# Seven block products in the second unit's first pair, row blocks loaded by SyncE, and a drain behind every two-source GpSimd operation

## The chip, the core and the metric

One core of a Trainium2 chip. The metric is the device time of one execution in microseconds. The kernel before took 782.65 us (median of three runs, 782.61 to 783.22). Engines are named as in the profile: PE is TensorE's matmuls and PEld its weight loads, DVE is VectorE, ACT is ScalarE, POOL is GpSimd, SP is SyncE.

## What is computed

Linear attention over 4 batches of 576 rows, then a token-mixing term and a feed-forward layer with a residual, then a routed mixture of experts:

```python
x = attention(q, k, v, w_phi)                       # (4, 576, 512)
u = x + (x.transpose(0, 2, 1) @ U @ V).transpose(0, 2, 1)
x = u + relu(u @ w_ch1) @ w_ch2                     # 512 -> 2048 -> 512
out[b, s] = p[e] * (relu(x[b, s] @ w1[e]) @ w2[e])  # e: the expert of row s
```

The experts are chosen for each row by a router, but all rows of a batch are first computed with the batch's own most frequent expert, and a loop at the end of the program repairs what differs.

## The kernel before

Everything is kept transposed: features on partitions, rows along the free axis. Each float32 operand of the large products is split into a rounded part and a remainder, and a product is three matmuls (part by part, part by remainder, remainder by part). The split costs a ScalarE cast and a subtraction (a two-source operation) for each tile: `w_end` does it for weights (a `w` tile of 128 x 2 x 512), `x_end` for rows (an `x` tile of 128 x 2 x 2 x 384). There are 14 `w` tiles, 9 `x` tiles and 8 `row` buffers for values that are not split yet.

**Items.** The feed-forward layer has 2048 hidden features in four units of 512 (`ffn_units`, `u.g` from 0 to 3), and its 2304 rows are three pairs of blocks of 384 rows (`NP` is 3). An item is one unit with one pair: items 0 to 2 are unit 0, 3 to 5 unit 1, 6 to 8 unit 2 (pairs in reverse), 9 to 11 unit 3 (`nf` is 12). Eight items of the expert layer follow. Item 0 runs inside the attention part, which ends at about 206 us. An item has two halves: the first product into `psf` (L971 to L973) with relu, and the second one, `mm2` (L1087 to L1089), whose result is added to `y` (L943).

**Two ways for the first half.** `plain_steps` multiplies the four 256 x 256 blocks A11 to A22 of the unit's weights with the four blocks B11 to B22 of the pair's rows: eight block products of 12 matmuls. `seven_steps` forms the same result from seven block products of 12 matmuls, in the order A11 B11, S2 T2, S1 T1, S3 T3, A22 T4, A12 B21, S4 B22. The S are sums of blocks of weights (`w_seven`), the T sums of blocks of rows (`x_sums`). After the products VectorE adds and subtracts in PSUM (`add`, through `dve`, L943, with the buffers `u2` and `u3`) ahead of relu. In the kernel before, items 4 to 11 use seven products; items 1 and 2 and also item 3 (`i == NP`, "flat") use eight.

**Where rows come from.** `x_plain` splits blocks of `y`; some are kept in DRAM (`xd`). `x_sums` loads four blocks of unsplit rows from `ud` with SyncE, makes the four T by eight subtractions of 384 elements and splits them (`x_end`). `x_load` brings split tiles back from `xd`, on GpSimd's DMA queue (L578). `x_next` says what each item prepares: item 2 loads the four plain blocks of pair 0 for item 3; items 3, 4 and 7 run `x_first` (B11, the sums, then B21 and B22) for the item behind them; items 5, 8 and 10 load all seven tiles.

**Where weights come from.** `raw_dma` loads 64-bit raw blocks with SyncE (L305) into two buffers, `narrow` turns them into float32 with six VectorE operations (L89 to L102) and one addition in two halves on GpSimd, `sums` makes the S, `w_end` splits.

**The planner.** The program is emitted in one order, by a planner in Python that keeps a clock for each engine (`free`), books a price for each operation (`cost`) and lets preparing work in (`gate`, `either`, `pump`) where its clock is at most a slack ahead of PE's. `either` chooses GpSimd or VectorE for a two-source operation. `spawn` gives a thread of work a due item; threads that are due first, and among these the earlier ones, go first. Each engine then runs its own instructions in the emitted order.

**Drains.** `paused` (L69 to L73) emits a two-source operation and, on GpSimd and under two conditions, a drain of that engine: `pauses[0]`, true for items 0 to 2 and from item 10 on (L1240), and GpSimd's clock being past the landing of the last DMA that `x_load` put on its queue (`landed`).

Of the kernel before, what the change touches and what calls it, by code (L numbers as in the profile page):

```python
# [8 lines left out]
F32R = mybir.dt.float32r  # L9
# [14 lines left out]
TW = 384  # L24
# [15 lines left out]
def model(ctx, tc, kq, vx, wphi, ident, up, vp, wff, wg, wmoe1, wmoe2, rconst, outT):  # L40
# [26 lines left out]
    landed, wire = [0.0], [0.0]  # L67

    def paused(eng, **kw):  # L69

        eng.tensor_tensor(**kw)  # L71
        if eng is nc.gpsimd and pauses[0] and free["POOL"] >= landed[0]:
            nc.gpsimd.drain()  # L73
# [94 lines left out]
    def cost(eng, n):  # L168
        return {"DVE": (0.075 + n / 960) * 1.15, "ACT": 0.17 + n / 1330, "POOL": 0.05 + n / 340}[eng]
# [123 lines left out]
    order = [(u, n) for u in ffn_units for n in (SEVEN if u.g > 1 else PLAIN)]  # L293
# [84 lines left out]
    def w_seven(u, get, free_, eng, p, due, flat=False):  # L378

        def end(s, f, back=None):  # L380
            spawn("w", due + (flat and s[0] == "S"), w_end(u, s, f, eng, back))
# [5 lines left out]
        if flat:  # L387
            a11 = yield from get("A11")
            end("A11", a11)
            a12 = yield from get("A12")  # L390
            end("A12", a12)
            a21 = yield from get("A21")
            end("A21", a21)
            a22 = yield from get("A22")
            end("A22", a22)
            s3 = yield from take(rows)
            yield from sums(p, s3, a11, a21, ALU.subtract)
            end("S3", s3, rows)
            yield from done("A21")
            yield from sums(p, a21, a21, a22, ALU.add)  # L400
            yield from done("A22")
            free_.append(a22)
        else:
            a21 = yield from get("A21")
            a11 = yield from get("A11")
            s3 = yield from take(rows)
            yield from sums(p, s3, a11, a21, ALU.subtract)
            end("S3", s3, rows)
            end("A11", a11)
            a22 = yield from get("A22")  # L410
            yield from sums(p, a21, a21, a22, ALU.add)
            end("A22", a22, free_)
# [4 lines left out]
        if not flat:  # L417
            a12 = yield from get("A12")
            end("A12", a12)
# [6 lines left out]
    def w_ffn(u, due):  # L426
# [6 lines left out]
        if u.g > 1:  # L433
            spawn("w", due, fetch(u, SEVEN))
        def second():
            for s in VS:
                f = yield from get(s)
# [1063 lines left out]
```

## Time and profile before

| | us |
|---|---|
| median of three runs | 782.65 |
| lowest and highest | 782.61, 783.22 |
| the profiled execution | 781.76 |
| its span, first to last instruction | 779.70 |
| PE busy in the span | 763.8 |
| DVE busy | 482.7 |
| POOL busy | 362.2 |
| ACT busy | 300.7 |

The profile is of one execution, whose time is 0.89 us under the median. Its span leaves out 2.06 us before the first and after the last instruction. The granted clock of TensorE is 0.999 of full speed over the span. A view's times count from the span's start. Idle time of an engine is put ahead of the instruction that ended it, with the one that released it; a busy time contains what an operation waits for inside itself.

### The profile page before, as it was taken

How to read it: one execution, taken by the hardware profiler on the slowest of the kernel's cores; microseconds unless marked ns; L12 is line 12 of the kernel's file. 1: busy time of each engine (PE TensorE's matmuls, PEld its weight loads, DVE VectorE, ACT ScalarE, POOL GpSimd, SP SyncE). 2: the span in 40 equal slices, each digit the busy share in tenths (PEclk: the TensorE clock that was granted, in tenths of full speed). 3: DMA queues.
4: the chain of work that ended last, by engine and by line, in shares of the span. 5: the costliest groups of instructions: out<-in, count | busy, mean ns of one | idle time of the engine just before them, and what ended most of it. 6: DMA issues, size and time to landing. Idle time of an engine off the chain costs nothing.

```text
span 779.7 us, 19252 instructions
## 1 busy us (share of the span) xinstructions
PE 763.8 (98%) x7776; PEld 741.6 (95%) x7776; DVE 482.7 (62%) x921; ACT 300.7 (39%) x682; POOL 362.2 (46%) x463
## 2 busy tenths in 40 slices
PE   8999999999999999899999999999999999999997
PEld 6899988999999999898999999999999999999997
DVE  7899999742488779897796865255643632203212
ACT  6667777652322131212213122023365164333420
POOL 1212423112477567574278532003566777866612
PEclk9999999999999999999999999999999999999999
DMA  6434556222342727591634807442453433434201
GB/s 200 153 125 160 207 178 227 71 104 82 136 169 82 277 88 278 195 340 65 228 120 162 301 1 270 152 146 82 131 186 97 133 102 102 125 122 127 79 1 63
DMA packets 45115, 114.34 MB, mean 147 GB/s; under 512 B 5024, under 2 KB 21536, under 8 KB 45024
## 3 DMA queue, kind: packets, MB, share of 16 engines
q1 hardware_dynamic: 36416, 82.74, 30.9%
q0 software_dynamic: 5152, 26.89, 10.2%
q10 hardware_dynamic: 3456, 3.46, 1.3%
q8 instruction: 62, 1.02, 0.5%
q14 instruction: 29, 0.24, 0.1%
HBM read 81.47 MB, written 31.60 MB: 145 GB/s over the span
## 4 chain that ended last, share of the span: by engine, by line
PE 82%; DVE 9%; issue 4%; POOL 2%; ACT 2%; POOLq 0%; DMA 0%; DVEq 0%; ACTq 0%
PE psf L1087 11%; PE psf L1089 11%; PE psf L1088 11%; PE psf L972 11%; PE psf L971 11%; PE psf L973 10%; PE kv L709 4%; PE pj L676 3%; PE num L743 3%; PE tq L723 2%; POOL row L71 1%; PE tps L769 1%; PE utps L786 1%; DVE row L89 1%; DVE pg L680 1%
## 5 line engine op out<-in xcount | busy, mean ns | idle before, releaser
L1087 PE MATMUL psf<-hhi,w 128*128 128x384 f32 (+1 forms) x640 | 204.6, 320 | 1.6 <-DVE hlo L945 1.6
L1088 PE MATMUL psf<-hhi,w 128*128 128x384 f32 (+1 forms) x640 | 203.7, 318 | 0.0
L1089 PE MATMUL psf<-hlo,w 128*128 128x384 f32 (+1 forms) x640 | 203.6, 318 | 0.0
L971 PE MATMUL psf<-x,w 128*128 128x384 f32 (+1 forms) x608 | 194.2, 319 | 3.0 <-DVE u L943 3.0
L972 PE MATMUL psf<-x,w 128*128 128x384 f32 (+1 forms) x608 | 193.9, 319 | 0.0
L973 PE MATMUL psf<-x,w 128*128 128x384 f32 (+1 forms) x608 | 193.9, 319 | 0.0
L945 DVE SCALAR_TENSOR_TENSOR hlo<-psf,hhi 128x384 fp32r<-128x384 f32 (+1 forms) x160 | 78.9, 514 | 145.9 <-ACT hhi L959 145.6
L71 POOL TENSOR_TENSOR w<-row,w 128x256 fp32r<-128x256 f32 x122 | 97.3, 809 | 92.8 <-ACT w L344 39.1
L959 ACT ACTIVATE hhi<-psf 128x384 fp32r<-128x384 f32 (+1 forms) x160 | 70.3, 461 | 176.6 <-PE psf L973 85.3
L71 POOL TENSOR_TENSOR row<-row,row 128x256 f32<-128x256 f32 (+1 forms) x105 | 89.1, 869 | 99.4 <-DVE row L102 91.1
L1087 PEld LDWEIGHTS psf<-hhi,w 128*128 128x128 f32 x640 | 120.1, 188 | 3.4 <-DVE hlo L945 2.3
L943 DVE TENSOR_TENSOR y<-psf,y 128x384 f32<-128x384 f32 (+1 forms) x128 | 67.0, 528 | 86.0 <-PE psf L1089 82.0
L1088 PEld LDWEIGHTS psf<-hhi,w 128*128 128x128 f32 x640 | 120.1, 188 | 0.0
L1089 PEld LDWEIGHTS psf<-hlo,w 128*128 128x128 f32 x640 | 120.1, 188 | 0.0
L971 PEld LDWEIGHTS psf<-x,w 128*128 128x128 f32 x608 | 114.3, 188 | 4.9 <-DVE u L943 4.0
L972 PEld LDWEIGHTS psf<-x,w 128*128 128x128 f32 x608 | 114.2, 188 | 0.3 <-POOL x L71 0.3
L973 PEld LDWEIGHTS psf<-x,w 128*128 128x128 f32 x608 | 114.2, 188 | 0.0
L71 POOL TENSOR_TENSOR x<-y,x 128x288 fp32r<-128x288 f32 (+1 forms) x56 | 51.9, 930 | 85.2 <-ACT x L512 78.2
L71 POOL TENSOR_TENSOR w<-raw,w 128x256 fp32r<-128x256 f32 x72 | 54.5, 757 | 32.6 <-ACT w L344 16.1
L344 ACT CAST w<-row 128x512 fp32r<-128x512 f32 x61 | 36.3, 622 | 76.7 <-POOL row L71 31.5
L679 DVE TENSOR_REDUCE mx<-pj 128x6 f32<-128x768 f32 (+2 forms) x49 | 45.8, 935 | 5.8 <-PE pj L676 5.7
L680 DVE TENSOR_TENSOR pg<-pj,mx 128x768 f32<-128x768 f32 (+2 forms) x49 | 46.1, 941 | 2.5
(110 smaller groups left out, 950.3 us busy)
## 6 DMA issues: line engine op xcount, KB each, us to landing
x<-xd POOLq DMA_DIRECT2D x34, 768.0 KB, 6.4
xd<-x SPq DMA_DIRECT2D x22, 768.0 KB, 4.5
raw<-in_wff SPq DMA_DIRECT2D x32, 512.0 KB, 3.3
raw<-in_wmoe SPq DMA_DIRECT2D x37, 256.0 KB, 2.7
kq<-in_kq SPq DMA_DIRECT2D x14, 576.0 KB, 3.9
row<-in_wmoe SPq DMA_DIRECT2D x27, 256.0 KB, 2.9
vt<-in_vx SPq DMA_DIRECT2D x16, 325.0 KB, 3.3
ud<-y SPq DMA_DIRECT2D x4, 1152.0 KB, 6.8
```

Source lines behind the costliest of these rows:

```text
L71: eng.tensor_tensor(**kw)
L679: nc.vector.tensor_reduce(out=mx[:, :, sl], in_=ps[:, :, sl], axis=AX, op=ALU.max, apply_absolute_value=True)
L680: nc.vector.tensor_tensor(out=p[:, :, sl], in0=ps[:, :, sl], in1=mx[:, :, sl].unsqueeze(3).to_broadcast([128, 2, m, 128]), op=ALU.subtract)
L943: nc.vector.tensor_tensor(**kw)
L945: nc.vector.scalar_tensor_tensor(op1=op1, **kw)
L959: at = act(lambda: nc.scalar.activation(out=hhi, in_=src, func=ACTF.Relu), n_, ready)
L971: nc.tensor.matmul(ps, lhsT=w[:, 0, c], rhs=x[:, 0, k, :n_], start=(first and k == 0), stop=False, skip_group_check=True)
L972: nc.tensor.matmul(ps, lhsT=w[:, 0, c], rhs=x[:, 1, k, :n_], start=False, stop=False, skip_group_check=True)
L973: nc.tensor.matmul(ps, lhsT=w[:, 1, c], rhs=x[:, 0, k, :n_], start=False, stop=(stop and k == 1), skip_group_check=True)
L1087: nc.tensor.matmul(ps, lhsT=wh, rhs=hhi, start=(k == 0), stop=False)
L1088: nc.tensor.matmul(ps, lhsT=wl, rhs=hhi, start=False, stop=False)
L1089: nc.tensor.matmul(ps, lhsT=wh, rhs=hlo, start=False, stop=(k == 3))
```

## The change

- Item 3 uses seven block products: unit 1 fetches its blocks in the order `SEVEN`, `w_seven` loses its `flat` branch, and `w_ffn` spawns `fetch` for every unit and takes V0 to V3 behind the sums.
- Item 2 then runs `x_first` for item 3, and items 3 and 4 run it for the items behind them; item 7 loads all seven tiles of pair 0 where it ran `x_first`. B12 of pair 0 is no longer kept in `xd`.
- `x_load` issues on SyncE, without a gate on GpSimd's clock and with its transfer counted from PE's clock.
- A drain stands behind every two-source operation on GpSimd that goes through `paused` once attention is over (`pauses[0] = True`, without `landed`).
- The planner's price of GpSimd for n elements goes from 0.05 + n/340 to 1.05 (0.2 + n/340) us.

```diff
-        if eng is nc.gpsimd and pauses[0] and free["POOL"] >= landed[0]:
+        if eng is nc.gpsimd and pauses[0]:
             nc.gpsimd.drain()
...
-        return {"DVE": (0.075 + n / 960) * 1.15, "ACT": 0.17 + n / 1330, "POOL": 0.05 + n / 340}[eng]
+        return {"DVE": (0.075 + n / 960) * 1.15, "ACT": 0.17 + n / 1330, "POOL": (0.2 + n / 340) * 1.05}[eng]
...
-    order = [(u, n) for u in ffn_units for n in (SEVEN if u.g > 1 else PLAIN)]
+    order = [(u, n) for u in ffn_units for n in (SEVEN if u.g else PLAIN)]
...
-        if u.g > 1:
-            spawn("w", due, fetch(u, SEVEN))
-        def second():
-            for s in VS:
-                f = yield from get(s)
-                spawn("w", due, w_end(u, s, f, nc.gpsimd, rows))
-
-        if u.g == 1:
-            spawn("w", due, second())
-        yield from w_seven(u, get, rows, nc.gpsimd, nc.gpsimd, due, u.g == 1)
-        if u.g > 1:
-            yield from second()
+        spawn("w", due, fetch(u, SEVEN))
+        yield from w_seven(u, get, rows, nc.gpsimd, nc.gpsimd, due)
+        for s in VS:
+            f = yield from get(s)
+            spawn("w", due, w_end(u, s, f, nc.gpsimd, rows))
...
-            yield from x_end(key, s, y[:, k, t], key[0] == "p" and (s != "B12" or key[1] == 0))
+            yield from x_end(key, s, y[:, k, t], key[0] == "p" and s != "B12")
...
-            yield from gate("POOL", 0.6, x)
-            nc.gpsimd.dma_start(out=x, in_=xd[key[1]][XD.index(s)])
-            landed[0] = touched[id(x)] = max(transfer(768, free["POOL"]), touched.get(id(x), 0.0) + 4.5)
+            nc.sync.dma_start(out=f32(x), in_=f32(xd[key[1]][XS.index(s)]))
+            emitted[0] += 1
+            force[0] = False
+            touched[id(x)] = max(transfer(768), touched.get(id(x), 0.0) + 4.5)
...
-        return ("m" if u.kind == "moe" else "f" if u.g and i != NP else "p", b)
+        return ("m" if u.kind == "moe" else "f" if u.g else "p", b)
...
-        if i < NP:
-            return x_load(x_key(NP), BS) if i == NP - 1 else None
-        if i in (3, 4, 7):
+        if i < NP - 1:
+            return None
+        if i < 2 * NP - 1:
             return x_first(x_key(i + 1), i + 1)
...
-            if last[u] == i or i == NP and f // 2 == 1:
-                for k in range(2 if last[u] == i else 1):
+            if last[u] == i:
+                for k in range(2):
...
-        pauses[0] = i < NP or i > nf - NP
+        pauses[0] = True
...
-            flat = items[i][0].kind == "moe" or items[i][0].g == 0 or i == NP
+            flat = items[i][0].kind == "moe" or items[i][0].g == 0
...
-    spawn("w", 3, fetch(units[1], PLAIN))
     spawn("w", 3, w_ffn(units[1], 3))
```

## Rows read from the trace of the kernel before

**Rows 1.** The page: busy us, share and instructions of each engine; the chain's shares.

```profile
PE 763.8 (98%) x7776; PEld 741.6 (95%) x7776; DVE 482.7 (62%) x921; ACT 300.7 (39%) x682; POOL 362.2 (46%) x463
...
PE 82%; DVE 9%; issue 4%; POOL 2%; ACT 2%; POOLq 0%; DMA 0%; DVEq 0%; ACTq 0%
```

**Rows 2.** Windows: stretch, length, busy us (count) of five engines, clock, DMA share, GB/s.

```profile
205.95:272.65 66.70, 66.70 (x387) 66.70 (x385) 52.06 (x83) 17.85 (x33) 47.51 (x55) 1.00 0.53 193
...
239.35:255.98 16.63, 16.63 (x97) 16.63 (x97) 12.85 (x22) 5.68 (x11) 13.57 (x19) 1.00 0.23 76
255.98:272.65 16.67, 16.67 (x98) 16.67 (x97) 12.21 (x18) 1.80 (x4) 9.24 (x10) 1.00 0.86 310
272.65:289.28 16.63, 16.63 (x97) 16.63 (x97) 12.00 (x18) 4.31 (x9) 9.79 (x12) 1.00 0.30 103
...
305.95:322.78 16.83, 14.83 (x86) 14.40 (x85) 15.28 (x28) 3.16 (x8) 11.39 (x13) 1.00 0.83 321
...
339.50:356.52 17.02, 14.99 (x86) 14.36 (x85) 15.58 (x25) 4.35 (x10) 9.36 (x12) 1.00 0.81 316
...
404.76:420.26 15.50, 14.84 (x85) 14.52 (x85) 12.93 (x22) 4.12 (x9) 12.98 (x17) 1.00 0.66 210
...
468.15:482.70 14.55, 14.55 (x85) 14.55 (x85) 7.45 (x15) 3.90 (x9) 4.67 (x8) 1.00 0.70 230
```

**Rows 3.** PE's waits from 190 us on: us in total, times, longest.

```profile
PE psf L971 <- DVE u L943: 3.0, 3, 2.0
PE psf L1087 <- DVE hlo L945: 1.6, 1, 1.6
```

**Rows 4.** DVE in order of time: start, us, line, operation, shapes, count.

```profile
310.56 2.13 DVE L338 TENSOR_TENSOR w<-row,w 128x512 fp32r<-128x512 f32 x2
...
334.50 4.49 DVE L89 TENSOR_SCALAR row<-raw 128x512 uint32<-128x512 uint32 x1
...
342.41 0.42 DVE L89 TENSOR_SCALAR row<-raw 128x512 uint32<-128x512 uint32 x1
...
348.43 2.63 DVE L338 TENSOR_TENSOR w<-row,w 128x512 fp32r<-128x512 f32 x1
...
408.46 2.51 DVE L338 TENSOR_TENSOR row<-row,row 128x512 f32<-128x512 f32 x1 [0.88 <-POOL w L71]
```

**Rows 5.** POOL in order of time, 333 to 352 us, where no drains stand.

```profile
334.75 3.94 POOL L71 TENSOR_TENSOR x<-row,x 128x384 fp32r<-128x384 f32 x4
...
345.37 3.74 POOL L71 TENSOR_TENSOR w<-row,w 128x256 fp32r<-128x256 f32 x4
349.07 1.43 POOL L71 TENSOR_TENSOR row<-row,row 128x256 f32<-128x256 f32 x2
```

**Rows 6.** POOL in order of time, with drains; in brackets the idle time before.

```profile
223.25 0.74 POOL L71 TENSOR_TENSOR w<-row,w 128x256 fp32r<-128x256 f32 x1 [0.16 <-POOL w L71]
```

**Rows 7.** The drains, L73: shortest, median and longest in ns, first and last start.

```profile
L73 POOLq DRAIN  x228: 598/841/3462, 207.4 to 771.6; - x114
```

**Rows 8.** POOL in order of time around item 3, and one ACT cast of x.

```profile
263.97 1.88 POOL L71 TENSOR_TENSOR row<-row,row 128x256 f32<-128x256 f32 x2 [0.63 <-DVE row L102]
273.07 0.75 POOL L71 TENSOR_TENSOR w<-row,w 128x256 fp32r<-128x256 f32 x1 [7.21 <-ACT w L344]
...
278.15 2.00 POOL L71 TENSOR_TENSOR row<-row,row 128x384 f32<-128x384 f32 x2
285.06 5.17 POOL L71 TENSOR_TENSOR row<-row,row 128x256 f32<-128x256 f32 x5 [4.91 <-DVE row L102]
...
295.33 2.17 POOL L71 TENSOR_TENSOR x<-row,x 128x384 fp32r<-128x384 f32 x2
297.44 1.10 POOL L578 DMA_DIRECT2D x<-xd  x2
...
297.99 0.84 ACT L512 CAST x<-row 128x768 fp32r<-128x768 f32 x1 [5.83 <-POOL x L71]
```

**Rows 9.** DMA issues: count, KB each, median us from issue to landing.

```profile
x<-xd POOLq DMA_DIRECT2D x34, 768.0 KB, 6.4
```

More of the change, by code (lines that the diff above doesn't have):

```diff
@@ L66, in model @@
     pauses = [False]
-    landed, wire = [0.0], [0.0]
+    wire = [0.0]
     def paused(eng, **kw):
         eng.tensor_tensor(**kw)
-        if eng is nc.gpsimd and pauses[0] and free["POOL"] >= landed[0]:
+        if eng is nc.gpsimd and pauses[0]:
             nc.gpsimd.drain()
@@ L376, in sums, with w_seven @@
         both(eng, out, a, b, op)
-    def w_seven(u, get, free_, eng, p, due, flat=False):
+    def w_seven(u, get, free_, eng, p, due):
         def end(s, f, back=None):
-            spawn("w", due + (flat and s[0] == "S"), w_end(u, s, f, eng, back))
+            spawn("w", due, w_end(u, s, f, eng, back))
         def done(*names):
@@ L385, in done @@
                 yield "wait"
[L387 to L412, printed above, removed]
+        a21 = yield from get("A21")
+        a11 = yield from get("A11")
+        s3 = yield from take(rows)
+        yield from sums(p, s3, a11, a21, ALU.subtract)
+        end("S3", s3, rows)
+        end("A11", a11)
+        a22 = yield from get("A22")
+        yield from sums(p, a21, a21, a22, ALU.add)
+        end("A22", a22, free_)
         yield from done("A11")
@@ L416, in w_seven @@
         end("S2", a11)
-        if not flat:
-            a12 = yield from get("A12")
-            end("A12", a12)
+        a12 = yield from get("A12")
+        end("A12", a12)
         yield from done("A12")
@@ L494, in model @@
     BS = ("B11", "B21", "B12", "B22")
-    XD = XS + ("B12",)
     xo, xdone = {}, set()
-    xd = [dram.tile([8, 128, 2, 2, TW], F32R, name=f"xd{p}") for p in range(NP)]
+    xd = [dram.tile([7, 128, 2, 2, TW], F32R, name=f"xd{p}") for p in range(NP)]
     ud = dram.tile([128, 4, B * S], F32, name="ud")
@@ L517, in send @@
             def send():
-                nc.sync.dma_start(out=f32(xd[key[1]][XD.index(s)]), in_=f32(x))
+                nc.sync.dma_start(out=f32(xd[key[1]][XS.index(s)]), in_=f32(x))
                 if late:
@@ L1348, in model @@
     free.update(PE=0.0, DVE=0.0, ACT=1.0, POOL=2.0)
-    landed[0] = wire[0] = 0.0
+    wire[0] = 0.0
     touched.clear()
```

## The prediction

> **What bounds the kernel now.** I read the page's busy line and chain first. TensorE is busy 98% of the span and 82% of the chain that ended last is matmuls [rows 1]. So a change can gain in two ways only: fewer matmuls, or less time in which TensorE waits. The stretch of the change begins where attention ends, at about 206 us; from there the work is a list of items, one for each weight unit and pair of batches (items 0 to 2 unit 0, 3 to 5 unit 1, 6 to 8 unit 2, 9 to 11 unit 3, then the experts).
>
> The second view is a table of windows cut at item boundaries [rows 2]. A plain first half (96 matmuls, item 3, from 272.65) takes 16.63 us. An undisturbed first half with seven products (84 matmuls, item 9, from 468.15) takes 14.55 us. Three other seven-product halves are longer than that: item 4 (305.95) by 16.83 - 14.55 = 2.28 us, item 5 (339.50) by 17.02 - 14.55 = 2.47 us, item 7 (404.76) by 15.50 - 14.55 = 0.95 us, 5.7 us in all. The granted clock is 1.00 in each of these windows (the 2.4 GHz level), so the excess is waiting. The third view, TensorE's waits from 190 us on, has only two lines, and both name VectorE: L971 for the sums u (L943), and L1087 for hlo (L945) [rows 3]. VectorE is therefore what is late, in three items; GpSimd and the DMAs never are.
>
> The fourth view is VectorE's order of time just ahead of those waits [rows 4]. Ahead of item 5 a one-source operation that takes 0.42 us at 342.41 took 4.49 us at 334.50; inside it a two-source one took 2.63 us, and in item 7 one took 2.51 us. Beside the first lies a run of four GpSimd operations without a drain, 334.75 to 338.69; beside the second a run of four and one of two, 345.37 to 350.50 [rows 5]. VectorE's operation ends when the run ends. This is starvation. In item 4 it is different: two operations at 310.56 took 2.13 us together, about 1.06 each, so VectorE got in between, and its u sums came late because of the queue ahead of them, not because of one blocked operation.
>
> **The change part by part.**
>
> *Seven products in item 3.* Seven products of 12 matmuls replace eight: 16.63 - 14.55 = 2.08 us less of TensorE, on the path [rows 2]. The sum has -2.08.
>
> *Preparing item 3 earlier.* Unit 1 needs eleven w tiles in place of twelve (A21 itself goes), which saves one ScalarE cast and one subtraction that nobody waits for; I cost it at nothing, and it can't lose while ScalarE is busy only 17.85 of 66.70 us [rows 2]. The sums of A blocks already run before 272.65 in the kernel before: the last row<-row work on GpSimd ahead of item 3 ends at 265.85 [rows 8]. What really moves is the x side: the four loads of plain blocks for item 3 go, and instead the sums of pair 0 (four loads of rows, eight subtractions and eight remainders of 384 elements, four casts, four sends) move from item 7 into item 2. On GpSimd that is 16 operations at 1.00 us (the two at 278.15) [rows 8] plus 0.16 for each drain [rows 6]: 18.6 us. Over items 1 and 2 GpSimd is busy 47.51 of 66.70 us and VectorE 52.06 [rows 2], and GpSimd sits idle for 7.21 us right ahead of item 3 [rows 8]. So the work fits, with little over, if the planner gives VectorE a share. Item 7 loses the same work.
>
> *The price in item 3.* It becomes an item like item 4: seven-product sums on VectorE while pair 1's x sums and unit 2's blocks are prepared. I give it item 4's excess, 2.28 us. The bounds: nothing (item 9), and 4.75 us (item 4's and item 5's together). I take 2.28 because item 4 is the nearest row in what is done beside it, and it is also what a hurried x chain costs: T2 is wanted at 272.65 + 2.08 = 274.73, one product into the item; if GpSimd began at 265.85 and did nothing else, six subtractions at 1.16, a cast of 0.84 and two remainders at 1.16 end at about 276, 1 to 2 us late.
>
> *Drains everywhere.* They add 0.16 us between two GpSimd operations [rows 6], on an engine that is busy 9.79 of 16.63 us in item 3's first half [rows 2]; that is hidden, and where GpSimd is late nothing of TensorE waits for it today. With a gap behind each operation a VectorE operation should wait for one GpSimd operation (about 1.0 us), not four. The starved operations of rows 4 then give back about 3.0 + 1.0 us ahead of item 5 and 0.9 in item 7, more than the waits there, so I take both excesses as gone: -2.47 and -0.95 (item 7 also loses its x sums). Item 4 had no starvation and keeps its 2.28. What is late next there is still VectorE.
> The Trainium skill speaks against this (page "SBUF — State Buffer", section "Who interferes with whom"): the port pair that VectorE and GpSimd share is a lock held for one whole instruction, and whoever issues first has it. By that rule the loser waits one instruction whether a drain stands there or not. The trace agrees for item 4's pair at 1.06 us and disagrees at 334.50, where the wait covered four instructions. By the rule the sum would lack the -2.47; that is the second rival below.
>
> *Loads of row blocks on SyncE.* GpSimd loses 34 issues of about 0.55 us (1.10 for two at 297.44) [rows 8]; SyncE gains 37 (three more, since pair 0's finished sums are now loaded for item 8). They now queue behind weight loads that wait for VectorE, and behind each load wait the sends and weight loads after it. A load lands 6.4 us after issue in the middle [rows 9], and its tile is wanted half an item (some 15 us) later, so I cost the move at nothing; the bounds are a gain up to item 7's excess, already counted, and a loss of one late load, 6.4 us. It is what allows the drains at all: the longest drain took 3.46 us against 0.84 in the middle [rows 7], as one must when it waits for something else than the operation ahead of it.
>
> *GpSimd's price in the planner.* 512 elements go from 1.56 to 1.79 us in its books, so a few two-source operations move to VectorE. Between nothing and one more excess like item 4's; I count nothing apart from item 3's 2.28.
>
> **Sum.** -2.08 - 2.47 - 0.95 + 2.28 = -3.2 us. The profiled execution took 781.76 us (span 779.70 and 2.06 around it) and lies 0.89 below the median of 782.65; from 781.76 the sum is 778.5, which at the median is 779.4.
>
> **The rivals.**
> 1. *The stretch is clean.* Neither item 3 nor item 4 waits: -2.08 - 5.70 = -7.8, 774.9 us. For it: item 2, already drained for the most part, runs at 16.63 us, without a wait [rows 2]. Against: they have no seven-product sums on VectorE, and VectorE's queue grows.
> 2. *Drains buy nothing* (the lock rule, or a VectorE that is simply too full). Item 3 pays like item 5, and only item 7, rid of its sums, recovers: -2.08 + 2.47 - 0.95 = -0.6, 782.1 us. For it: item 4 waits without any starved operation. Against: 4.49 us beside four GpSimd operations.
> 3. *Pair 0's x sums come too late (slower).* Place: the second product of item 3, S2 by T2. GpSimd's work for unit 1 stands ahead of it in the planner's order and ends at 265.85. In the kernel before, the same chain took from 278.15 to about 296.4, until its second and third remainder of x were done (the first of the two at 295.33), 18.2 us [rows 8]. From 265.85 that gives 284.0, 9.3 us behind 274.73: -2.08 - 2.47 - 0.95 + 9.3 = +3.8, 786.4 us. It turns slower than before by 0.2% (1.6 us) when T2 is ready after 274.73 + 5.5 + 1.6 = 281.8 us on the clock of before. Against: that chain was in no hurry; GpSimd was idle for 4.91 us in it.
>
> **How the numbers follow.** A measurement of this kernel can tell about 0.2%, 1.6 us, from no change. The forecast, item 3's excess from 0 to 3.8 us: 777 to 781, chance 0.45. Clean: 0.13. Drains buy nothing: 0.20, nearly all of it within 0.2%. Late x sums: 0.22, 784 to 788. Faster: 0.45 + 0.13 + 0.02 = 0.60; same 0.18; slower 0.22. The range goes from the clean case, 775, to the greater part of the late one, 786; above it I leave about 0.1, below it less.
>
> **What would show it.** Matmuls of L971 to L973 drop by 12 in all (4 for each line). Item 3's first half: 14.55 us if clean, about 16.8 by the forecast, over 20 by the third rival. No one-source VectorE operation of 512 elements over 1.5 us between 270 and 470 us, if drains do what I think; if 2.5 us and more are still there, the second rival holds. No x<-xd on GpSimd's queue. Wrong altogether: TensorE waits that name a DMA x<-xd or GpSimd, or waits in the expert items, where I expect nothing to change.

## The result and the profile after

The changed kernel takes 789.0 us (median of 6 runs, 787.56 to 789.98); the kernel before took 782.82 us beside it (6 runs, 782.23 to 784.44). The ratio is 1.0073, interval 1.0058 to 1.0088: slower by about 0.7%, where I forecast 779.4 us and a range of 775 to 786. The profiled execution has a span of 785.7 us, 6.0 more than before.

From the page of the changed kernel: busy us, share and instructions of each engine, the chain's shares, and the loads of finished x tiles (count, KB, median us from issue to landing; [rows 9]).

```profile
PE 763.7 (97%) x7764; PEld 740.8 (94%) x7764; DVE 501.2 (64%) x967; ACT 301.1 (38%) x683; POOL 292.1 (37%) x360
...
PE 54%; POOLq 6%; issue 3%; DVE 1%; DMA 0%; DVEq 0%
...
x<-xd SPq DMA_DIRECT2D x37, 768.0 KB, 6.4
```

TensorE has the 12 matmuls less that the change promises (7776 in [rows 1]) and is busy for as long: 763.7 us against 763.8. VectorE has 46 operations and 18.5 us more, GpSimd 103 instructions and 70 us less. The drains now stand in the chain of work that ended last (POOLq). The 37 loads are on SyncE and land as they did.

Where the 6.0 us lie is seen in the same table of windows as [rows 2], cut at the changed kernel's own item boundaries. Columns: stretch, length, busy us (count) of PE, PEld, DVE, ACT and POOL, clock, DMA share, GB/s.

```profile
206.41:273.01 66.60, 66.60 (x387) 66.60 (x385) 47.26 (x81) 19.95 (x36) 40.06 (x44) 1.00 0.46 165
273.01:293.60 20.59, 15.90 (x85) 14.19 (x84) 19.05 (x29) 4.01 (x9) 14.39 (x14) 1.00 0.91 339
...
310.38:326.84 16.46, 14.72 (x86) 14.40 (x85) 14.14 (x26) 4.15 (x10) 10.24 (x13) 1.00 0.81 317
343.59:364.06 20.47, 16.39 (x85) 15.95 (x85) 16.97 (x28) 4.92 (x11) 15.19 (x17) 0.92 0.96 382
412.04:426.59 14.55, 14.55 (x85) 14.55 (x85) 11.94 (x24) 3.56 (x8) 3.81 (x5) 1.00 0.80 291
```

In items 1 and 2 together (206.41) VectorE is busy 47.26 us and GpSimd 40.06, each *less* than in [rows 2] (52.06 and 47.51), though pair 0's sums were to be formed there. Item 3's first half (273.01) takes 20.59 us: seven products cost 3.95 us *more* than the eight of before. Item 4 (310.38) is 0.37 us shorter than in [rows 2]. Item 5 (343.59) is 20.47 us, 3.46 longer. Item 7 (412.04) is clean at 14.55, 0.95 shorter. The small rest (both halves of item 6, the second halves of items 3 to 5) is -0.13. The sum is +5.96 us; from the start of item 1 to the second half of the last item the trace has +5.98 (561.35 us against 555.37). I compare kernels by that length where a microsecond matters, because item 1 itself starts anywhere between 205.90 and 208.85 us in the profiled executions of this study, with nothing changed ahead of it.

TensorE's waits in the changed kernel, 200 to 600 us: us in total, times, longest. [rows 3] had two lines.

```profile
PE psf L946 <- DVE u L918: 4.1, 1, 4.1
PE psf L1062 <- DVE hlo L920: 3.2, 2, 1.7
PE psf L947 <- DVE x L71: 2.6, 1, 2.6
PE psf L947 <- POOL x L71: 0.6, 2, 0.3
```

The two `x` lines are new and both lie in item 3: there the matmuls wait for pair 0's x sums. The two waits for hlo end item 3 (1.47 us) and item 4 (1.74 us). The 4.1 us for u lie in item 5. Two stretches of VectorE and GpSimd show what is behind each.

VectorE in order of time ahead of item 3 and in it, the changed kernel: start, us, line, operation, count, and in brackets the idle time before.

```profile
266.15 0.55 DVE L918 TENSOR_TENSOR y<-psf,y 128x384 f32<-128x384 f32 x1
271.51 0.56 DVE L71 TENSOR_TENSOR row<-row,row 128x384 f32<-128x384 f32 x1 [4.80 <-DMA row<-ud]
...
275.42 0.78 DVE L89 TENSOR_SCALAR row<-raw 128x512 uint32<-128x512 uint32 x1
276.23 1.13 DVE L92 TENSOR_SCALAR row<-row 128x512 f32<-128x512 f32 x1
...
279.74 0.68 DVE L102 SCALAR_TENSOR_TENSOR row<-raw,row 128x512 f32<-128x512 uint32 x1
280.33 1.56 DVE L71 TENSOR_TENSOR x<-row,x 128x384 fp32r<-128x384 f32 x2
```

GpSimd, same kernel and columns.

```profile
271.55 1.40 POOL L71 TENSOR_TENSOR row<-row,row 128x384 f32<-128x384 f32 x1 [1.97 <-DMA row<-ud]
...
276.07 1.01 POOL L71 TENSOR_TENSOR x<-row,x 128x384 fp32r<-128x384 f32 x1 [0.16 <-issue]
280.56 0.91 POOL L71 TENSOR_TENSOR row<-row,row 128x256 f32<-128x256 f32 x1 [3.48 <-DVE row L102]
```

**The late x sum.** The third product of item 3 needs T1. GpSimd makes one of its two remainders (276.07). The other is the first of the pair on VectorE at 280.33 (the second of that pair belongs to T3), behind a whole block of unit 2 being decoded (L89 at 275.42 to L102 at 279.74); TensorE waits 2.6 us for it. GpSimd stands idle for 3.48 us of the same time: what it has next in its order needs that decoded block. Neither engine is full; their orders cross.

**The hole.** At 271.51 VectorE comes back from 4.80 us in which it did nothing. It stood at the subtraction for T4, whose fourth row block was not there. SyncE's part of the order, same kernel, around that load and around the same load for the next pair:

```profile
267.74 0.38 SPq L518 DMA_DIRECT2D row<-ud  x1
...
340.55 0.38 SPq L518 DMA_DIRECT2D row<-ud  x1
```

The load is issued when a row buffer comes free, which a narrow addition on GpSimd frees (it ends at 267.72 and at 340.52, 0.02 and 0.03 us ahead of the issues), and the subtraction begins 3.8 and 4.0 us after the issue. The planner had put the subtraction where it expected the data. The second of these holes, 5.26 us up to 344.56, begins ahead of item 5 and ends 0.97 us into it:

```profile
338.75 0.55 DVE L918 TENSOR_TENSOR y<-psf,y 128x384 f32<-128x384 f32 x1
344.56 0.56 DVE L71 TENSOR_TENSOR row<-row,row 128x384 f32<-128x384 f32 x1 [5.26 <-DMA row<-ud]
```

Behind it the u sums are 4.1 us late.

### The profile page after: what moved, and what is told of

It is laid out like the page before. It is cut to its first block, busy times and chain, and to the rows that moved or that the text cites. A ratio compares the mean times of both kernels' runs of the same rounds, so it can differ in the third digit from the quotient of the medians.

```text
span 785.7 us, 19205 instructions
## 1 busy us (share of the span) xinstructions
PE 763.7 (97%) x7764; PEld 740.8 (94%) x7764; DVE 501.2 (64%) x967; ACT 301.1 (38%) x683; POOL 292.1 (37%) x360
## 3 DMA queue, kind: packets, MB, share of 16 engines
q10 hardware_dynamic: 3456, 3.46, 1.3%
## 4 chain that ended last, share of the span: by engine, by line
PE 54%; POOLq 6%; issue 3%; DVE 1%; DMA 0%; DVEq 0%
PE psf L1062 9%; PE psf L1063 9%; PE psf L1064 9%; PE psf L946 8%; PE psf L947 8%; PE psf L948 8%; POOLq L73 6%; PE psf L1107 1%; DMA row<-ud 0%; PE psf L1161 0%; PE psf L1114 0%; DVE y L918 0%; DVE row L95 0%; DVE row L97 0%; DVE row L99 0%
## 5 line engine op out<-in xcount | busy, mean ns | idle before, releaser
L71 POOL TENSOR_TENSOR row<-row,row 128x256 f32<-128x256 f32 (+1 forms) x90 | 75.1, 838 | 142.9 <-DVE row L102 129.3
L71 POOL TENSOR_TENSOR w<-row,w 128x256 fp32r<-128x256 f32 x98 | 80.6, 825 | 83.3 <-ACT w L368 37.9
L71 POOL TENSOR_TENSOR x<-y,x 128x288 fp32r<-128x288 f32 (+1 forms) x51 | 47.7, 940 | 145.1 <-ACT x L486 131.7
L71 POOL TENSOR_TENSOR w<-raw,w 128x256 fp32r<-128x256 f32 x44 | 33.0, 750 | 42.2 <-PE psf L948 23.0
```

## The experiments

### Each part by itself

**Seven products alone.** The changed kernel with the three other edits taken back (cut: the condition on `landed`, the gate and the bookings go back with them).

```diff
-        return {..., "POOL": (0.2 + n / 340) * 1.05}[eng]
+        return {..., "POOL": 0.05 + n / 340}[eng]
...
-        pauses[0] = True
+        pauses[0] = i < NP or i > nf - NP
...
-            nc.sync.dma_start(out=f32(x), in_=f32(xd[key[1]][XS.index(s)]))
+            nc.gpsimd.dma_start(out=x, in_=xd[key[1]][XS.index(s)])
```

> The seven products in item 3 with everything else as before: row blocks loaded by GpSimd, drains only in items 0 to 2 and from item 10 on, the old price of GpSimd. Theory (VectorE is held at the head of its queue by the fourth load of unsplit rows, for T4, which it gets because of GpSimd's new price; 4.8 us in item 2 and 5.3 us in item 4 of the changed kernel): those two holes are absent or on GpSimd, item 3 costs about what item 4 cost before, the time is 781 to 784 us. Rival A (the seven products overload items 2 and 3 whatever the rest does): item 3 stays near 20 us in its first half, 786 to 789 us.

**All but the seven products.** The kernel before with the price, the drains and the SyncE loads of the change (cut in the same way).

```diff
-        return {..., "POOL": 0.05 + n / 340}[eng]
+        return {..., "POOL": (0.2 + n / 340) * 1.05}[eng]
...
-        pauses[0] = i < NP or i > nf - NP
+        pauses[0] = True
...
-            nc.gpsimd.dma_start(out=x, in_=xd[key[1]][XD.index(s)])
+            nc.sync.dma_start(out=f32(x), in_=f32(xd[key[1]][XD.index(s)]))
```

> Item 3 plain as before; SyncE loads the row blocks, drains everywhere, the new price. Theory (hole ahead of T4's subtraction): item 3 is clean at 16.6 us, but the hole for pair 2's sums in item 4 can still be there and cost item 5 up to 6 us; 782 to 786 us. Rival A (the products are the whole cost): 778 to 780 us. Rival B (drains or SyncE's queue are the cost): 785 to 788 us with waits spread over items 3 to 8.

**SyncE loads alone**, the last pair of lines of that diff, and **SyncE loads with drains everywhere**, the last two pairs, both at the old price.

> The kernel before with one part of the change: SyncE issues the loads of row blocks (item 3 plain, old price, drains as before in items 0 to 2 and from item 10 on, without the condition on a landing, which no load sets any more). If the queue of SyncE holds the rows back, item 3 or the later items wait and it is slower by 1 to 4 us; if the move is free, as forecast, 781 to 784 us.

> The kernel before with SyncE's loads and with drains everywhere, still at the old price. By the forecast drains end the starvation of VectorE (no operation of 512 elements over 1.7 us in items 3 to 8) and give back about 3 us against the kernel before: 778 to 781 us. If drains buy nothing: 782 to 785 us, and the difference between this and the kernel with the new price as well belongs to the price.

Measured, with the first halves of items 3, 4, 5 and 7 from the profiled execution (clean is 14.55 with seven products, 16.64 with eight), all in us:

```
kernel         median   ratio to before [95%]     item 3   item 4   item 5   item 7
before         (1)                                16.64    16.83    17.01    15.50
seven_alone    793.31   1.0134 [1.0113, 1.0156]   23.69    15.49    21.52    16.58
rest_alone     783.66   1.0005 [0.9993, 1.0017]   16.64    16.44    20.18    14.55
after          789.0    1.0073 [1.0058, 1.0088]   20.59    16.46    20.47    14.55
sp_alone       779.08   0.9928 [0.991, 0.9946]    16.64    16.50    14.55    14.55
sp_and_drains  780.41   0.995 [0.9932, 0.9968]    16.64    17.33    14.57    14.55
(1) 782.82 to 784.02 us beside the others; each ratio is to the runs of before on the same chip
```

The seven products cost 10.4 us by themselves; SyncE loads gain 5.6 us by ratio (4.05 by the length from item 1 on); drains on top of them gain nothing (the intervals overlap). seven_alone (793.31) and sp_alone (779.08) both lie outside everything that I had expected of them. With the price in, the whole SyncE gain is gone: rest_alone stands where the kernel before stands, and its item 5 has 20.18 us. Taking the differences of these ratios as shares of 783 us, the change is -5.6 (SyncE loads), +6.0 (price and drains, 1.0005 - 0.9928) and +5.3 (seven products on top, 1.0073 - 1.0005): +5.7. By the length from item 1 on the three are -4.05, +5.58 and +4.46.

The drains and the copies that GpSimd makes further down aren't booked by the planner: in the traces, kernels that differ in these alone (sp_alone and sp_and_drains, after and after_few_drains) run the same operations in the same order on VectorE, GpSimd and ScalarE. The price is another matter. The pages of sp_and_drains and of rest_alone, which differ in the price alone:

```profile
PE 763.4 (98%) x7776; PEld 742.5 (95%) x7776; DVE 470.6 (60%) x912; ACT 300.5 (39%) x682; POOL 350.4 (45%) x440
```

```profile
PE 764.3 (98%) x7776; PEld 743.2 (95%) x7776; DVE 494.6 (63%) x955; ACT 300.9 (38%) x682; POOL 297.8 (38%) x366
```

VectorE gets 43 operations and 24.0 us more.

### The hole in front of T4

**Old price in the changed kernel**, the first pair of lines of the first diff, and **few drains in the changed kernel**, the second pair.

> The changed kernel with GpSimd's old price in the planner (0.05 + n/340), so that fewer two-source operations go to VectorE. Theory: T4's subtraction goes to GpSimd, VectorE's two holes shrink to under 1 us and the time falls to 781 to 784 us. Rivals A and B: the price is not the matter, 787 to 790 us.

> The changed kernel with drains only in items 0 to 2 and from item 10 on, as before; price and loads stay changed. Theory: the plan is the same, so the holes stay: 786 to 790 us. Rival B (drains are the cost): 782 to 784 us. If drains help as I forecast, it is slower than the changed kernel by 1 to 3 us, with VectorE operations over 2 us in items 3 to 5.

**T4's subtraction on GpSimd only**, in the changed kernel and in rest_alone (cut: the lines that pass the engine on to `either`):

```diff
-        yield from sub(got["B21"], got["B22"], got["B21"])
+        yield from sub(got["B21"], got["B22"], got["B21"], "POOL")
```

> The changed kernel, but the planner may put T4's subtraction (the one that waits for the fourth load of rows) on GpSimd alone. Theory: VectorE's holes of 4.8 us ahead of item 3 and 5.3 us ahead of item 5 are gone (under 1 us), item 5's first half falls from 20.5 to 15 to 17 us, item 3's from 20.6 to 16 to 19; 779 to 784 us. Rival A (too much work for VectorE in items 2 to 5): the holes go, but the waits of TensorE stay, since the same work is still to be done; 787 to 790 us.

> Item 3 plain, SyncE's loads, drains everywhere, the new price, and T4's subtraction on GpSimd alone. Theory: the only large wait of that kernel, 5.6 us in item 5, shrinks to at most 2 us: 778 to 781 us, faster than before. Rival A: item 5 stays at 19 to 20 us and the time at 783 to 785 us.

**Four microseconds more booked for the landing of the fourth row load**, in the changed kernel, in rest_alone, in rest_alone with few drains, and in sp_alone:

```diff
-            touched[id(r)] = max(transfer(384), touched.get(id(r), 0.0) + 3.5)
+            touched[id(r)] = max(transfer(384), touched.get(id(r), 0.0) + 3.5) + 4.0 * (s == "B21")
```

> The changed kernel, with 4 us more booked for the landing of the fourth load of rows, so that the planner puts T4's subtraction later on whichever engine it takes. Theory: same as with GpSimd alone in item 4 (item 5's first half 15 to 17 us), but item 3, where T4 is wanted at once, may stay late; 781 to 786 us. Rival A: 787 to 790 us.

> Item 3 plain, SyncE's loads, drains everywhere, the new price, and 4 us more booked for the fourth load of rows. Theory: no hole on VectorE, item 5's first half at 14.6 to 16.5 us, 778 to 781 us. Rival A: 783 to 785 us.

> The fastest kernel so far (item 3 plain, SyncE's loads, the new price, 4 us more booked for the fourth load of rows), with drains only in items 0 to 2 and from item 10 on. If the drains are what ended the starvation: VectorE operations over 2 us again and 780 to 783 us. If the new price (a plan with more room on GpSimd) ended it: the same as with drains, 778 to 779.5 us.

> The kernel before with SyncE loads alone, and 4 us more booked for the fourth row load. If the hole at the fourth subtraction is what is left of the waits there: item 4's first half falls from 16.5 to about 15 us and the time is 777 to 778.5 us. If VectorE's queue is what is left: no change, 778.5 to 779.5 us.

The last column is the longest idle time of VectorE or GpSimd, 200 to 600 us, that the landing of a row load ended.

```
kernel                 median   ratio to before [95%]     item 3   item 4   item 5   longest hole, engine
after                  789.0    1.0073 [1.0058, 1.0088]   20.59    16.46    20.47    5.26 VectorE
after_old_price        785.6    1.0033 [1.0023, 1.0043]   21.29    17.86    14.56    3.56 GpSimd
after_few_drains       787.71   1.0054 [1.0033, 1.0074]   20.28    16.48    18.35    5.06 VectorE
after_t4_pool          791.59   1.0115 [1.0091, 1.0139]   24.11    15.76    20.49    4.37 GpSimd
after_t4_later         785.75   1.0033 [1.0021, 1.0045]   24.37    15.25    15.78    2.03 GpSimd
rest_alone             783.66   1.0005 [0.9993, 1.0017]   16.64    16.44    20.18    5.04 VectorE
rest_t4_pool           781.29   0.9976 [0.9962, 0.999]    16.64    16.47    17.93    4.10 GpSimd
rest_t4_later          778.81   0.9941 [0.9923, 0.9959]   16.64    18.50    14.55    3.90 GpSimd
rest_later_few_drains  779.81   0.9946 [0.9924, 0.9967]   16.64    17.02    14.55    3.79 GpSimd
sp_alone               779.08   0.9928 [0.991, 0.9946]    16.64    16.50    14.55    2.84 GpSimd
sp_t4_later            781.31   0.9981 [0.9967, 0.9995]   16.64    16.75    15.57    2.01 GpSimd
```

One booked number takes item 5 from 20.47 to 15.78 us and from 20.18 to 14.55: in these two kernels VectorE's hole was its cause. The price doesn't do it by VectorE's load alone, since rest_t4_later has the new price too. The 21.52 us of item 5 in seven_alone are another case: no such hole is there, VectorE waits 4.36 us for GpSimd (up to 345.04, L92), and no run takes that wait away. A hole on GpSimd hurts only where VectorE or TensorE needs what stands behind it: rest_t4_later has one of 3.90 us ahead of its plain item 3, which is clean. TensorE's waits in rest_t4_later, 200 to 600 us, are one line, in item 4:

```profile
PE psf L972 <- DVE u L944: 2.1, 1, 2.1
```

The price makes the hole, not the drains: with few drains and the new price it is there (5.06), with drains everywhere and the old price item 5 is clean (sp_and_drains, 14.57). Putting the subtraction on GpSimd only moves the hole there: item 5 gets back 2.25 us in rest_t4_pool and nothing in after_t4_pool, where item 3 gets worse (24.11). And the booked number is no cure in itself: in sp_alone, where VectorE has no hole, it does nothing good (0.9981, not the 777 to 778.5 us that I expected). Each edit of a price or a booking makes the planner lay out the whole stretch anew; only where a named hole went can I say what was gained.

### Item 3: pair 0's x sums

**No sums of pair 0.** after_t4_later with pair 0's four row sums left out; its tiles are filled by loads of one finished tile.

```diff
-            nc.sync.dma_start(out=f32(x), in_=f32(xd[key[1]][XS.index(s)]))
+            nc.sync.dma_start(out=f32(x), in_=f32(xd[key[1]][XS.index("B11" if key[1] == 0 and s[0] == "T" else s)]))
...
-            return x_first(x_key(i + 1), i + 1)
+            return x_load(x_key(i + 1)) if i == NP - 1 else x_first(x_key(i + 1), i + 1)
```

> The changed kernel with 4 us more booked for the fourth load of rows, and with the row sums of pair 0 left out: T1 to T4 of pair 0 are not formed, the stored tile of B11 is loaded in their place, in items 3, 8 and 9. Everything else of item 3, its seven products and VectorE's additions behind them, is as in the changed kernel. Theory (the sums of pair 0, which fall into item 2 and 3, are what item 3 waits for): item 3's first half falls from 24 us to 14.6 to 16.5 us and the time to 775 to 779 us. Rival (VectorE's additions of seven products, beside unit 1's last weights and unit 2's first, are too much by themselves): item 3 stays over 18 us, 780 to 786 us.

Its total (1087.1 us) says nothing, since tokens then go to other experts and the end of the kernel repeats expert work (8276 matmuls against 7764); it is read by windows, items 3 and 4:

```profile
273.97:288.52 14.55, 14.55 (x85) 14.55 (x85) 12.47 (x25) 4.01 (x9) 7.47 (x8) 1.00 0.57 213
305.19:319.75 14.56, 14.56 (x86) 14.56 (x86) 11.41 (x23) 5.01 (x11) 10.22 (x14) 1.00 0.86 300
```

against the same window of after_t4_later, with the sums:

```profile
273.27:297.64 24.37, 18.00 (x86) 16.72 (x86) 19.09 (x33) 5.47 (x12) 16.13 (x17) 0.86 0.86 317
```

The sums are what item 3 pays for, all 9.8 us of it (6.4 us of waits, four of them, and matmuls slowed by the clock, which is at 0.50 from 288 to 294 us); without them item 4 is clean too, and the stretch is what I called "clean" in the first rival. The blocks of unit 1 are in time.

**The sums one item earlier** (begun in item 1 in place of item 2), with the 4 us booked, at the old price with few drains and at the new price with drains everywhere.

```diff
-        if i < NP - 1:
-            return None
+        if i < NP:
+            return x_first(x_key(NP), NP) if i == 1 else None
```

> The changed kernel with 4 us more booked for the fourth row load of a pair, the old price of GpSimd and the few drains, and pair 0's x sums begun one item earlier (in item 1 in place of item 2). Theory that item 3 is only late: its first half falls from 24.4 us to 14.6 to 17 us, and the time is 774 to 778 us. Theory that item 3 lacks capacity (GpSimd and VectorE can't form pair 0's sums and the block sums in items 1 and 2 at all): its first half stays over 20 us, or item 2 grows by as much, and the time is over 783 us.

> The same with the price of GpSimd and the drains as the changed kernel has them. If item 3 is only late: first half 14.6 to 17 us and 775 to 779 us. If it lacks capacity: over 20 us, over 784 us. If price and drains matter beside that, this one is 1 us or more over its twin with the old price.

Measured: 780.46 us (ratio 0.9964, 0.9954 to 0.9975) at the new price, 790.68 us (1.0097, 1.008 to 1.0114) at the old. Item 3's window in the first and in the second:

```profile
274.52:291.62 17.10, 14.83 (x86) 14.37 (x85) 15.48 (x27) 4.27 (x10) 10.90 (x13) 1.00 0.51 189
```

```profile
272.50:298.12 25.62, 18.14 (x85) 17.19 (x85) 21.33 (x34) 4.62 (x10) 21.59 (x24) 0.80 0.44 155
```

At the new price the earlier start takes item 3 from 24.37 to 17.10 us, with items 1 and 2 still clean: the two engines *can* form these sums in time. So it is the order, not the capacity, that made them late. At the old price the order comes out badly in another way. TensorE's waits there, 200 to 600 us:

```profile
PE psf L946 <- DVE u L918: 6.4, 1, 6.4
```

This is its longest line of four, and no x sum is in them; VectorE stands at two steps of a block decode, 1.07 and 1.50 us, until GpSimd has done with w tiles, and the u sums queue behind them. The 10 us between the twins are far more than the 1 us that I had expected, and I can't split them between price and drains, since no run has one without the other here. Even the good twin doesn't earn the seven products: item 3 takes 17.10 us where eight products take 16.64, and 553.59 us from item 1 on against 553.24 for rest_t4_later without them.

### What held VectorE up

In the kernel before, the five VectorE operations over 1.7 us between 272 and 468 us are those of [rows 4] (4.49, 2.63, 2.51) and two of 2.38 and 2.27. I put the first three down to missing drains [rows 5]. What I hadn't looked at is GpSimd's line of time just ahead of the two runs of [rows 5], the kernel before:

```profile
333.64 1.10 POOL L578 DMA_DIRECT2D x<-xd  x2
...
344.26 1.10 POOL L578 DMA_DIRECT2D x<-xd  x2
```

Both runs come right behind two DMA issues by GpSimd itself (334.75 and 345.37 are their first operations). Three kernels test that: sp_alone with a DMA that GpSimd issues beside each load, from DRAM to a DRAM tile that nobody reads, of 768 KB, of 96 KB, and of 96 KB with drains everywhere.

```diff
             nc.sync.dma_start(out=f32(x), in_=f32(xd[key[1]][XD.index(s)]))
+            junk = dram.tile([16, 2, 2, TW], F32R, name=f"junk{next(serial)}")
+            nc.gpsimd.dma_start(out=junk, in_=xd[key[1]][XD.index(s)][:16])
```

> The kernel before with the row-block loads on SyncE (779.1 us when it ran alone), and beside each such load GpSimd issues one more DMA of the same 768 KB from DRAM to a DRAM tile that nobody reads (work that isn't part of the computation). Theory: it is GpSimd's issuing of DMAs that holds VectorE up; then one-source VectorE operations of 512 elements over 2 us are back near these issues (four or five of them in 272 to 468 us, as in the kernel before, against a longest of 1.40 us without the issues), items 5 or 7 wait again, and the time is 781 to 784 us. Rival: VectorE gained because the loads wait in another order, and GpSimd's issuing does nothing; then no such operation is over 1.6 us and the time stays at 779 to 780 us.

> As the kernel with the big copies of GpSimd, but each copy is 96 KB in place of 768 KB, so that it adds one eighth of the traffic (the copies aren't part of the computation). There, and in the kernel before, every one-source VectorE operation over 2 us lay beside GpSimd operations without drains that came right behind an issue of GpSimd; runs of up to eight such operations with no issue ahead of them held VectorE up for no more than 1.4 us. Theory: the issue is what matters, not the traffic; two to five operations over 2 us are back, and the time is 780 to 783 us. Rival: the traffic held VectorE up; then no operation is over 1.6 us and the time is 779 to 780 us.

> The same small copies in the kernel with SyncE loads and drains everywhere. If a drain between the operations behind an issue lets VectorE in (my first theory, for runs behind an issue): no one-source operation of 512 elements over 1.6 us, where the kernel without these drains has some over 2 us, and 780 to 782 us. If the lock is held by the issue itself, drains don't help: operations over 2 us here too, and 782 to 785 us. Drains that wait for the copy to land would show as drains of 1 us and more.

The big copies give 798.4 us (1.0193), the small ones 780.89 (0.996, 0.9946 to 0.9973), the small ones with drains 794.71 (1.0135, 1.0115 to 1.0155). The first of these times isn't the cost of issuing alone: with their traffic VectorE also waited 5.5 us for a raw weight load and GpSimd 6.1 us for a row block. The rows tell more. GpSimd and VectorE with the small copies:

```profile
332.30 0.99 POOL L583 DMA_DIRECT2D junk<-xd  x2
333.31 3.91 POOL L71 TENSOR_TENSOR x<-row,x 128x384 fp32r<-128x384 f32 x4
```

```profile
335.36 2.15 DVE L89 TENSOR_SCALAR row<-raw 128x512 uint32<-128x512 uint32 x1
```

The same place in the kernel with the big copies has 4.42 us, at 345.08 beside a run from 345.29. Over all runs of two and more GpSimd operations without drains between them, 272 to 468 us, split by whether a DMA issue of GpSimd ends within 0.2 us ahead of the run (worked out from the traces: how many runs, with less than 0.1 us between operations, and the longest VectorE operation beside them in us):

```
kernel          no issue ahead        right behind an issue
before          26 runs, 1.39         6 runs, five of them with 2.27 to 4.49
seven_alone     24 runs, 1.43         5 runs, 2.29, 1.78, 1.65, 1.16, 1.11
sp_alone        26 runs, 1.40         none
sp_plus_dummy   21 runs, 1.40         6 runs, 4.42, 2.61, 2.21 and three to 1.11
sp_small_dummy  26 runs, 1.40         4 runs, 2.15, 1.90, 1.12, 1.05
```

Of these 123 runs with no issue ahead, 90 have a VectorE operation beside them that works on SBUF alone, and VectorE gets in between: beside seven undrained operations from 292.46 us in sp_alone four of its operations take 1.12 to 1.40 us. Behind an issue it can be shut out until the run ends. In eleven of the 21 such runs a VectorE operation takes 1.90 us or more, and each of these ends 0.29 to 0.56 us after the run's last GpSimd operation; in two of the eleven (345.37 in the kernel before, 355.87 in sp_plus_dummy) two shorter ones had got in before it.

That doesn't show how much of the SyncE gain comes from here. sp_small_dummy has sp_alone's order of operations and the issues back, and its items 5 and 7 stay clean (14.56 and 14.55); it loses 1.16 us against sp_alone by the length from item 1 on, in item 4 (17.68 against 16.50). sp_alone itself has another order than the kernel before, with 9 VectorE operations less (912 against 921). So 2.89 of the 4.05 us are still there with small copies issued by GpSimd, and I can't split the gain further between the order and the issues.

With drains VectorE is shut out for one operation. VectorE and GpSimd in drains_small_dummy:

```profile
339.29 1.88 DVE L95 TENSOR_SCALAR row<-row 128x512 uint32<-128x512 uint32 x1
```

```profile
338.78 1.05 POOL L583 DMA_DIRECT2D junk<-xd  x2 [0.51 <-issue]
339.84 1.03 POOL L71 TENSOR_TENSOR x<-row,x 128x384 fp32r<-128x384 f32 x1
343.52 1.12 POOL L71 TENSOR_TENSOR x<-row,x 128x384 fp32r<-128x384 f32 x1 [2.64 <-PE psf L1093]
```

VectorE's operation spans the rest of the issue and the one operation behind it, 1.88 us, not four. But the drain behind that operation then takes until 343.42: it waits for GpSimd's own copy, whose landing is at 343.30 (the drains that end at 356.19 and 448.93 have a copy landing at 356.07 and 448.81). The drains of this kernel and of sp_and_drains (L73: shortest, median, longest in ns):

```profile
L73 POOLq DRAIN  x366: 529/842/6557, 209.6 to 786.6; - x183
```

```profile
L73 POOLq DRAIN  x366: 537/839/3524, 209.3 to 770.4; - x183
```

So a drain does what I said it does where it is dear: behind a DMA issue it costs GpSimd up to 6.56 us, and items 4, 5 and 8 of that kernel take 18.52, 22.50 and 18.86 us. Where the loads are on SyncE there is little for it to do: without it, in sp_alone, the longest VectorE operation from 272 to 468 us takes 1.40 us.

## Why the prediction was wrong, step by step

- *What bounds the kernel: VectorE, in items 4, 5 and 7.* Right for the kernel before. I concluded too much from "GpSimd and the DMAs never are": the waits of TensorE name the last engine of a chain, and the change put a DMA (T4's row block) and GpSimd at the head of one. The waits of VectorE itself show it, not those of TensorE.
- *Seven products, -2.08.* Right as a price: 14.55 us is reached wherever nothing is late (no_sums_t4_later). Here it was buried.
- *Preparing item 3 earlier, and its price of 2.28.* This step failed. "So the work fits, with little over" was true of the busy times (early_new_price shows it), but busy time says nothing of when an in-order engine gets to an operation. Measured in the changed kernel: 20.59 - 14.55 = 6.04 us, of which TensorE's waits for x are 3.2 us and the one for hlo behind them 1.47. The bound that I gave, 4.75 us, was too low too. It was taken from items whose x sums had been in place or unhurried, and the nearest row of a hurried chain, the 18.2 us of [rows 8], was set aside on the ground that it "was in no hurry; GpSimd was idle for 4.91 us in it". That idle time was the evidence: GpSimd stood there for VectorE, as at 280.56 now (3.48 us).
- *The third rival* was the right one, in its place a product later (T1 in the third product, 2.6 us, rather than T2 in the second), and with a price of 9.3 us, more than the 6.04 of the changed kernel and near the 9.1 and 9.8 of seven_alone and after_t4_later. (Its chain of 18.2 us ends with the second remainder, at 296.34; the third, which the text takes in, ended at 297.50.) Its total, 786.4, came within 2.6 us by luck, because two errors met: too much for item 3 (9.3), and item 5 counted as cured.
- *Drains everywhere, -2.47 and -0.95.* The sizes are right and the cause is wrong. Items 5 and 7 lose 2.46 and 0.95 us in sp_alone, in which no drain is added: the loads' move to SyncE does it. The three operations that I blamed on missing drains (4.49, 2.63 and 2.51 us) stood beside runs right behind GpSimd's issues. Whether they were what items 5 and 7 waited for is not shown either, since both items stay clean in sp_small_dummy. The second rival, that drains buy nothing, holds for the drains as the change uses them; sp_and_drains is no faster than sp_alone. Beside undrained runs with no issue ahead no VectorE operation took over 1.43 us; behind an issue 4.42 us cover four instructions. The Trainium skill's rule in "SBUF — State Buffer", section "Who interferes with whom" (whoever issues first holds the shared ports for one whole instruction), fits the first and not the second.
- *Loads on SyncE, at nothing.* This step failed, on the good side: 4.05 us by the trace and 5.6 by the ratio. Its bounds were "a gain up to item 7's excess" and a late load; no load was late in sp_alone (5.9 us from issue to landing in the middle, against 6.4 in [rows 9]). The half-sentence that the move "is what allows the drains at all" was right: 6.56 us for a drain beside GpSimd's own copies.
- *GpSimd's price, at nothing.* This step failed. I had a few operations move to VectorE; it was 43, in a new order, and the subtraction for T4 came to stand ahead of its data, on VectorE: +5.6 us in item 5 (20.18 against 14.57, rest_alone and sp_and_drains), the whole gain of the SyncE loads. My bound, one more excess like item 4's, was less than half of that.
- *What would show it.* "Over 20 us by the third rival" came true in item 3 (20.59). "No one-source VectorE operation over 1.5 us if drains do what I think" came true, and misled: with drains and with few drains alike the longest is 1.24 us (after, after_few_drains). A sign that two causes share tells nothing between them. TensorE waits naming x on GpSimd, my mark of "wrong altogether", are there with 0.6 us.

In one line: -5.6 for loads that I had at zero, +6.0 for a price that I had at zero and drains that I had at -3.4, and +5.3 for seven products that I had at +0.2.

The version to keep is sp_alone, the kernel before with SyncE loads and nothing else of the change: 779.08 us, 0.9928 of before (0.991 to 0.9946). rest_t4_later (0.9941, 0.9923 to 0.9959) can't be told from it.

## What to carry to other kernels

Before giving an engine more work, ask in which place of its order the new work stands and what in front of it waits for another engine or a DMA: the idle time inside the nearest like chain is a price, not a reserve. When one engine's operation is stretched, look at what the other engine did just *before* the overlap, not only during it, and ask whether the kernel waits for that operation at all: with two of them back, items 5 and 7 stayed clean. Where a planner writes the order, a change of one price is an edit of the whole order: read the waits of the in-order engines after it (a hole before one operation), and book the landing of a DMA by its issue time in the trace.

## What the runs showed of the hardware

**A wait can cost more than its length.** Item 5 of the changed kernel lost 5.92 us to one wait of 4.08. Windows across that wait, same columns as above:

```profile
343.59:349.60 6.01, 6.01 (x36) 6.01 (x36) 4.09 (x8) 2.63 (x5) 4.46 (x4) 1.00 1.03 412
349.60:354.00 4.40, 0.39 (x3) 0.07 (x1) 4.23 (x8) 0.62 (x1) 2.95 (x4) 1.00 1.00 409
354.00:356.00 2.00, 1.94 (x7) 1.94 (x8) 1.97 (x4) 0.00 (x0) 1.60 (x3) 0.59 1.00 412
356.00:358.00 2.00, 2.00 (x9) 2.00 (x8) 1.93 (x3) 0.00 (x0) 1.71 (x2) 0.56 1.08 357
358.00:360.00 2.00, 2.00 (x13) 2.00 (x13) 1.97 (x4) 0.00 (x0) 1.22 (x3) 1.00 0.95 377
```

The granted clock is 1.00 (2.4 GHz) up to the wait and falls after it, to 0.59 and 0.56 in two windows of 2 us, most of which is the 1.2 GHz level. The twelve matmuls from 354.06 to 357.82 take 3.76 us where twelve at the full clock take 2.08 (14.55 us for 84): 1.7 us on top of the wait, which with it makes 5.8 of the 5.92. Behind the wait of 2.6 us in item 3 the clock stayed at 1.00; behind the 6.4 us of early_old_price it was at 0.50 for three windows of 2 us. In after_t4_later it fell to 0.50 too, where no wait is longer than 2.4 us but four come close together (0.3, 1.6, 2.4 and 2.1). The excesses of [rows 2] had no such part, so an excess is not a measure of a wait, nor the other way round.

**GpSimd's DMA issue and VectorE.** As told above: in 11 of 21 runs of undrained GpSimd operations right behind an issue a VectorE operation was shut out until the run ended (4.49 and 4.42 us at most); beside the 123 other runs none took over 1.43 us. What in the issue does it stays open. It isn't the traffic alone, since copies of an eighth of the bytes did it too (2.15 and 1.90 us), and not each issue does it: beside three of the other ten runs VectorE had nothing to do on SBUF alone, but beside four, all in seven_alone, it got in after one or two operations (1.78 us at most). VectorE operations with a PSUM tile among their operands were never held up beside any of these runs: 412 of them took 0.57 us at most.
